# A hand-made list schedule with another rule for an engine's own results, new durations and a new set of urgencies

## The chip, the cores and the metric

The kernel runs on one core of a Trainium2 chip. The metric is the device time of one execution in microseconds. Of the kernel before, three runs gave 725.88, 728.35 and 729.00 us, so the median is 728.35 us. The profiled execution, from which all durations below come, took 728.77 us. Its span from the first to the last instruction is 727.0 us, and 1.77 us lie around it.

## What is computed

A packed attention feeds a feed-forward layer with an ELU in the middle. There are 8 batches, 8 heads, 576 tokens and 64 elements a head. 32 packed queries per head attend to the keys and values, and then the 576 queries attend to the packed result. The layer has 512 inputs, 2048 hidden units and 512 outputs, over all 4608 tokens.

```python
p_packed = sm_attn(p, k, v)                # softmax(scale * p k^T) v
out = sm_attn(q, p_packed, p_packed)
x = out.transpose(0, 2, 1, 3).reshape(B * S, H * D)
h = x @ w_in
g = np.where(h > 0.0, h, np.exp(np.minimum(h, 0.0)) - 1.0)
return g @ w_out
```

The inputs are float32, and the two weight matrices arrive as 64-bit words, which the kernel converts itself.

## The kernel before, in words

**The mathematics as it is tiled.** The second attention has only 32 keys a head, so the kernel multiplies its packed values with `w_in` first (`mstep`, matmuls on L800, evacuated as a high part on ScalarE and a low part on VectorE). The hidden layer of a token window is then a product of the softmax weights `a` with that `m`, both kept as a high and a low part, three matmuls for one product. The hidden matmuls stand on L1297 and L1304 (ordinary path) and on L1035 (Strassen path). ScalarE takes relu and exp of the result, VectorE joins them to the ELU, and the result `g` is split into a high and a low part again, for the output matmuls.

**Windows and steps.** Each batch has two windows. One takes 256 tokens, the other 320, of which 64 are kept aside as a leftover (`hb`) and written to memory. The leftovers of batches 0 to 3 and of 4 to 7 are read back later as two further sets of pairs ("rest"), beside the two windows of batch 7. A step is one window with one of the 16 slices f of 128 hidden units. The list `VISITS` says in which order batches 0 and 1 go through their steps, so that the first steps need only the first weights. A visit is a run of steps whose output is accumulated in PSUM. When it ends, the sums are copied out and stored, by an adding transfer of GpSimd's queue (L1447) where an earlier visit has stored already. From batch 2 on every window is one run of 16 steps. Counted so, batches 0 and 1 are steps 0 to 63, window (2, 0) is steps 64 to 79, and (2, 1) is steps 80 to 95.

**Two paths to the output.** Ordinary steps multiply a slice of `g` with its slice of `w_out` in six matmuls of 512 columns (L1400, L1401, L1403). From the window named in `S_FIRST` on, two slices go together as a pair, and a Strassen scheme does the pair with seven products in place of eight: 21 matmuls of 256 columns (L1191) where the ordinary way takes 12 of 512. For it VectorE forms sums of blocks of `g` (`sums`, three adds on L1117) and splits seven blocks and not four (L1126). The window's sums are put together at its end by a chain of VectorE adds (L1222). Sums of weight blocks are needed too: `strassen_weights(u)` makes them once for each of the eight pairs u (VectorE on L923, L929, L936, L939 and L956, casts on L308), stores them in memory, and each Strassen pair loads its four tiles again, 256 KB each. A pair named in `S_PLAINS` for its window is done the ordinary way with 12 matmuls inside the Strassen path.

**Who sets the order.** All work is declared as operations with an engine, a duration, dependencies, the buffers taken, and a number `prio`, which is a step plus or minus an offset. `schedule()` is a list scheduler. It keeps a clock of its own, and at each moment starts the ready operation of the lowest `prio` whose engine and buffers are free. The order that comes out is the program: every engine runs its instructions in that order, and the queue of SyncE (SP) issues its transfers in that order. The durations in the declarations have no other effect. `GAP` shortens the time for which an engine is taken, `LAG` lengthens the time until a result may be used. A result used by a later operation that can only run on the same engine counted as ready when that engine was free again, and every other result at its end with `LAG`.

**The offsets that the change touches.** `LI`, `LO` and `LM` say how many steps ahead of its first use a slice of `w_in`, a slice of `w_out` and an `mstep` become urgent. `FIRST` gives the order of the very first loads; the loads of k, v and q of one batch are chained in that order, and three weight slices fit in the staging ring. `T_ATT`, `T_ATT1`, `T_ATTS` time the six stages of a batch's attention, `TM` and `TMS` its four msteps, `T_S2` the second softmax half of batch 0. `T_SW` and `T_SW7` time the Strassen weights, `T_SL` the loads of their tiles, `T_SE` the adds at a window's end, `T_RL` and `T_RX` the loads and the output matmuls of the rest pairs, `T_HS` the stores of the leftovers. `LOOK` and `LOOK_S` say how many steps the output matmuls trail the hidden ones, and `STAY` how long PE stays with one kind of matmul.

Of the kernel before, what the change touches and what calls it, by code (L numbers as in the profile page):

```python
# [20 lines left out]
def packed_attention_elu_ffn(  # L21
# [51 lines left out]


    VISITS = [
# [4 lines left out]
    ]  # L80
    T_ATT = [8.5, 13.5, 10.5, 15.0, 16.0, 18.5]
    T_ATT1 = [-13.5, -9.5, -13.0, -6.5, -4.5, -13.5]
    LI = 6.5
    LO = 1.0
    LM = 3.0
    LOOK = 3.25
    TM = [22.5, 23.5, 25.0, 22.5]
    FIRST = "i3 i0 o0 k i2 v o1 q".split()
    T_S2 = 2.0
    STAY = 8  # L90
    SWITCH = 0.105
    F_PLAIN = 0
    H_PLAIN = [0, 1]
    T_WS = 33
    T_AS = 7
    S_PLAIN = []
    S_PLAINS = {
        (2, 0): [1], (2, 1): [0, 7], (3, 0): [4], (3, 1): [0], (4, 0): [0], (4, 1): [1],
        (5, 0): [], (5, 1): [0], (6, 0): [1], (6, 1): [1],
    }  # L100
    T_SW7 = 17
    T_ATTS = {3: [-3, 1.5, -4, 5, 12.5, 21.5], 4: [5.5, 5, 13.5, 8.5, 11.0, 25.5], 5: [-0.5, 0.5, -1.5, 6.5, 12.5, 21.0], 6: [5, 8.0, 14.5, 4.5, 17.0, 27.0], 7: [-4, -2, -2.5, 3, 14.5, 22.0]}
    TMS = {3: [21, 25, 25.5, 26.5], 4: [21.5, 19.5, 27.0, 27.0], 5: [23, 29, 33.0, 24.0], 6: [26.0, 15.5, 25.0, 27.0], 7: [19, 31, 30.0, 30.5]}
    T_RL = 7.0
    T_RX = 2.0
    T_HS = 29.0
    S_FIRST = (2, 0)
    T_SW = 17.5
    T_SL = 14.5
    T_SE = 12.5  # L110
    LOOK_S = 5.5

    class Ring:
# [47 lines left out]
        pass  # L161

    ops = []
    GAP = {"PE": 0.0, "DVE": -0.08, "ACT": -0.1, "DMA": 0.0, "POOL": 0.0, "CTL": 0.0}
    LAG = {"PE": 0.2, "DVE": 0.05, "ACT": 0.05, "DMA": 2.2, "POOL": 5.0, "CTL": 0.0}

    def op(prio, on, fn, deps=(), take=(), use=(), after=(), mode=None, lag=0):
        o = Op()
        o.lag = lag
        o.prio, o.on, o.fn, o.deps = prio, on, fn, [d for d in deps if d is not None]  # L170
        o.after = [d for d in after if d is not None]
        o.take, o.end, o.n, o.mode = list(take), None, len(ops), mode
        for b in list(take) + list(use):
            b.users.append(o)
        ops.append(o)
        return o

    def schedule():

        for o in ops:  # L180
            o.wait, o.ready, o.next = len(o.deps) + len(o.after), 0.0, []
        for o in ops:
            for d in o.deps:
                d.next.append((o, True))
            for d in o.after:
                d.next.append((o, False))
        todo = sorted(ops, key=lambda o: (o.prio, o.n))
        idle_at = {e: 0.0 for e in GAP}
        now, out, mode, converted = 0.0, [], None, 0
        conv = set(conv_ops)  # L190

        def engine_for(o):

            if o.wait or o.ready > now:
                return None
            for r in {id(b.ring): b.ring for b in o.take}.values():
                if not r.grant([b for b in o.take if b.ring is r], now):
                    return None

            spare = 2.0 * (converted < len(conv_ops))  # L200
            e = min(o.on, key=lambda e: max(idle_at[e], now) + o.on[e] + spare * (e == "DVE"))
            return e if idle_at[e] <= now else None

        while todo:
            for n, o in enumerate(todo[:400]):
                if o.wait or o.ready > now:
                    continue
                e = engine_for(o)
# [12 lines left out]
                idle_at[e] = now + cost + GAP[e]  # L221
                o.start, o.end = now, now + cost + LAG[e] + o.lag
                for x, needs in o.next:
                    x.wait -= 1
                    if needs:

                        x.ready = max(x.ready, idle_at[e] if list(x.on) == [e] else o.end)
                for r in {id(b.ring): b.ring for b in o.take}.values():
                    r.take([b for b in o.take if b.ring is r], now)
                out.append((o, e))  # L230
                todo.remove(o)
                converted += o in conv
                break
            else:
                ends = [o.end for o, _ in out[-400:] if o.end > now]
                ends += [t for t in idle_at.values() if t > now]
                assert ends, [(o.prio, o.on) for o in todo[:20]]
                now = min(ends)
        return out
# [168 lines left out]
    def attention(b, ts):  # L408
# [20 lines left out]
        if whole:  # L429
            x = ("k0", "q0")[b]  # L430
# [63 lines left out]
        for name, fn, bufs, t in (  # L494
# [12 lines left out]
        ld_k, ld_v, ld_q = lds["k"], lds["v"], prev_ld  # L507
        st.ld_q = ld_q
        e1T, tr_done = [], []
# [80 lines left out]
        o4s, o, t, free = [], None, ts[0], prev_b.tmp_last if b > 1 else None  # L590
        if b < S_FIRST[0] + 1:
            o1 = op(t, {"PE": 1.0}, s1, ld_k, take=ps1 + e1s, use=[p_b] + k_b, after=[free], mode=1)
            for g in range(G):
                o = op(t, {"DVE": 0.76}, lambda e, g=g: smax1(e, g), [o1], use=[ps1[g]], after=[o])
# [4 lines left out]
        else:  # L599
            kept, o1 = [], None  # L600
            for half in range(2):
# [9 lines left out]
                    t, {"ACT": 0.4}, lambda e, half=half, ps=ps, g=g: keep(e, half, ps, g), [o1],  # L611
                    use=[ps, e1s[g]],
                ) for g in range(G)]
            o = op(t, {"DVE": 0.26}, neg_both, [o])
            for g in range(G):
                o4s.append(op(
                    t, {"ACT": 0.9}, lambda e, g=g: sexp1_flat(e, g), [o] + kept[g::G], use=[e1s[g]],
# [40 lines left out]
                            start=(c == 0), stop=(c == NKC - 1),  # L658
                        )

        o = op(ts[2], {"PE": 0.85}, pv, ld_v + tr_done, take=[ps, pp_b], use=v_b + e1T, mode=2)
        done = []
        for g in range(G):
            def norm(e, g=g, ps=ps):
# [250 lines left out]
    def strassen_weights(u):  # L915
# [31 lines left out]
               w_split.get(f), w_split.get(f + 1)], take=[w_b, t_b], after=[run["w8"]])  # L947
        run["w8"] = x
        x = op(prio, {"DVE": 0.62}, t13, [x], use=[w_b, t_b])
        x = op(prio, {"DVE": 0.7}, t24, [x], use=[w_b, t_b])  # L950
        for n, b in enumerate(sw):
            def high(e, n=n, b=b):
                copy(e, b.t[:, :H], cut(t_b, n))
# [50 lines left out]
    def strassen_pair(i, b, win, f):  # L1004
# [128 lines left out]
            return g_b.all[:, x0:x0 + P]  # L1133

        if not plain:
            done = [op(i + 1, {"DVE": 0.95}, sums, done, use=[w8])]
        x = run["g"] = op(
            i + 1, {"ACT": 0.62 if plain else 0.95}, hi, done, take=[g_b], use=[w8], after=[run["g"]]
        )
# [359 lines left out]
```

## Time and profile before

| | |
|---|---|
| median of three runs | 728.35 us (725.88 to 729.00) |
| profiled execution | 728.77 us |
| its span | 727.0 us |
| PE busy | 680.1 us, 6060 matmuls |
| VectorE (DVE) busy | 610.8 us, 1311 instructions |
| ScalarE (ACT) busy | 460.4 us, 892 instructions |
| bytes moved | 167.80 MB, 231 GB/s mean |
| granted TensorE clock | 0.994 mean |

PE is the row of matmuls and PEld that of their weight loads. The profile's stretches give, for a piece of the span, each engine's busy time and the granted clock; the difference to the length of the piece is what the engine was idle. Matmuls overlap one another in the pipeline, so a matmul's own duration is longer than the distance to the next one, and the distance of starts is what it costs. Numbers in square brackets behind a row of the timeline are the idle time of that engine just ahead of it, and the instruction that ended it.

### The profile page before, as it was taken

How to read it: one execution, taken by the hardware profiler on the slowest of the kernel's cores; microseconds unless marked ns; L12 is line 12 of the kernel's file. 1: busy time of each engine (PE TensorE's matmuls, PEld its weight loads, DVE VectorE, ACT ScalarE, POOL GpSimd, SP SyncE). 2: the span in 40 equal slices, each digit the busy share in tenths (PEclk: the TensorE clock that was granted, in tenths of full speed). 3: DMA queues.
4: the chain of work that ended last, by engine and by line, in shares of the span. 5: the costliest groups of instructions: out<-in, count | busy, mean ns of one | idle time of the engine just before them, and what ended most of it. 6: DMA issues, size and time to landing. Idle time of an engine off the chain costs nothing. (4 is left out here: it accounts for less than half of the span.)

```text
span 727.0 us, 16122 instructions
## 1 busy us (share of the span) xinstructions
PE 680.1 (94%) x6060; PEld 592.3 (81%) x6060; DVE 610.8 (84%) x1311; ACT 460.4 (63%) x892; POOL 16.9 (2%) x24
## 2 busy tenths in 40 slices
PE   3698998999999999999999999999999999899996
PEld 2456777777779888898889889998799879899996
DVE  4899887999998987869977987879987989677874
ACT  6688999875777556655564567655564565454441
POOL 0000011010120000000000000000000000000000
PEclk9999999999999999999999999999999999999999
DMA  9856569388589976687778867997787758665763
GB/s 344 279 196 184 174 195 234 77 226 270 123 238 284 315 245 200 211 267 255 232 260 262 287 197 223 289 306 256 252 259 259 246 156 282 177 211 159 267 217 117
DMA packets 102799, 167.80 MB, mean 231 GB/s; under 512 B 26177, under 2 KB 35393, under 8 KB 102465
## 3 DMA queue, kind: packets, MB, share of 16 engines
q1 hardware_dynamic: 100128, 162.04, 68.8%
q0 software_dynamic: 2592, 4.72, 4.4%
q8 instruction: 48, 0.79, 0.4%
q14 instruction: 31, 0.25, 0.1%
HBM read 139.98 MB, written 26.74 MB: 229 GB/s over the span
## 5 line engine op out<-in xcount | busy, mean ns | idle before, releaser
L1191 PE MATMUL psum<-sw,g 128*128 128x256 f32 x1224 | 185.8, 284 | 0.3 <-DVE part L1222 0.3
L1191 PEld LDWEIGHTS psum<-sw,g 128*128 128x128 f32 x1224 | 162.7, 190 | 8.0 <-issue 7.4
L308 ACT CAST g<-w 128x896 fp32r<-128x896 f32 (+1 forms) x96 | 87.1, 907 | 77.9 <-DVE w L1117 59.2
L1126 DVE TENSOR_TENSOR g<-w,g 128x896 fp32r<-128x896 f32 (+1 forms) x96 | 100.0, 1044 | 28.0 <-ACT g L308 27.0
L1035 PE MATMUL psum<-a_hi,m_hi 128*128 128x256 f32 (+1 forms) x384 | 117.1, 305 | 6.6 <-DVE hb L1042 5.0
L1035 PE MATMUL psum<-a_lo,m_hi 128*128 128x256 f32 (+1 forms) x384 | 113.4, 295 | 0.0
L1035 PE MATMUL psum<-a_hi,m_lo 128*128 128x256 f32 (+1 forms) x384 | 113.4, 295 | 0.0
L1191 PE MATMUL psum<-wo_a,g 128*128 128x256 f32 (+1 forms) x552 | 93.2, 300 | 2.0 <-DVE hb L1042 2.0
L1117 DVE TENSOR_TENSOR w<-w 128x128 f32<-128x128 f32 (+1 forms) x258 | 86.8, 336 | 8.4
L1035 PEld LDWEIGHTS psum<-a_hi,m_hi 128*128 128x128 f32 x384 | 72.6, 189 | 20.6 <-issue 8.1
L1191 PEld LDWEIGHTS psum<-wo_a,g 128*128 128x128 f32 x552 | 78.3, 191 | 8.5 <-issue 3.6
L1191 PE MATMUL psum<-wo_b,g 128*128 128x256 f32 (+1 forms) x516 | 81.5, 286 | 0.0
L1191 PEld LDWEIGHTS psum<-wo_b,g 128*128 128x128 f32 x516 | 70.5, 189 | 3.5 <-issue 1.8
L1035 PEld LDWEIGHTS psum<-a_lo,m_hi 128*128 128x128 f32 x384 | 72.7, 189 | 0.2
L1035 PEld LDWEIGHTS psum<-a_hi,m_lo 128*128 128x128 f32 x384 | 72.6, 189 | 0.0
L1047 ACT ACTIVATE e<-psum 128x320 f32<-128x320 f32 x96 | 41.9, 436 | 39.3 <-PE psum L1035 34.3
L1042 DVE SCALAR_TENSOR_TENSOR w<-e,psum 128x256 f32<-128x256 f32 x96 | 39.8, 415 | 15.0 <-ACT e L1050 14.4
L1047 ACT ACTIVATE w<-psum 128x512 f32<-128x512 f32 x48 | 28.7, 597 | 29.5 <-PE psum L1035 12.7
L1050 ACT ACTIVATE e<-e 128x320 f32<-128x320 f32 x96 | 45.3, 471 | 2.9
L800 PE MATMUL psum<-w_in_sb,ppT 64*32 64x512 f32 (+1 forms) x640 | 36.1, 523 | 5.5 <-DVE w_in_sb L357 3.7
L813 DVE TENSOR_TENSOR m_lo<-psum,m_hi 128x1024 fp32r<-128x1024 f32 (+1 forms) x36 | 37.3, 1041 | 4.5 <-ACT m_hi L308 4.3
L1042 DVE SCALAR_TENSOR_TENSOR w<-w,psum 128x512 f32<-128x512 f32 x48 | 32.7, 682 | 9.8 <-ACT w L1050 9.3
(121 smaller groups left out, 1150.0 us busy)
## 6 DMA issues: line engine op xcount, KB each, us to landing
sw<-sw_dram SPq DMA_DIRECT2D x344, 256.0 KB, 3.7
raw<-in_w_in SPq DMA_DIRECT2D x16, 512.0 KB, 4.1
raw<-in_w_out SPq DMA_DIRECT2D x16, 512.0 KB, 5.1
kvq<-in_v SPq DMA_DIRECT2D x16, 512.0 KB, 5.2
out<-part SPq DMA_DIRECT2D x32, 256.0 KB, 3.1
sw_dram<-sw SPq DMA_DIRECT2D x32, 256.0 KB, 5.8
kvq<-in_kT SPq DMA_DIRECT2D x14, 576.0 KB, 4.9
kvq<-in_qT SPq DMA_DIRECT2D x14, 576.0 KB, 5.8
```

The lines of the kernel that those rows point to most:

```text
L308: (nc.scalar.copy if e == "ACT" else nc.vector.tensor_copy)(out=out, in_=in_)
L800: nc.tensor.matmul(ps.t[cols_of(pair), g, :w], lhsT=st.ppT.t[rows_of(g), pair, :], rhs=w_in_sb[rows_of(g), pair, c * FC + part * w:c * FC ...
L813: nc.vector.tensor_tensor(out=m_b[1].t[:, :, fs], in0=ps.t[:, :, :w], in1=m_b[0].t[:, :, fs].bitcast(F32), op=ALU.subtract,)
L1035: nc.tensor.matmul(ps, lhsT=m_b[p].t[:, g, o:o + P], rhs=st.a.t[q][:, g, cols], start=(n == 0), stop=(n == 3 * G - 1),)
L1042: nc.vector.scalar_tensor_tensor(out=out, in0=e_, scalar=-1.0, in1=ps, op0=ALU.add, op1=ALU.max)
L1047: nc.scalar.activation(out=out, in_=ps, func=AF.Relu, scale=-1.0)
L1050: nc.scalar.activation(out=x, in_=x, func=AF.Exp, scale=-1.0)
L1117: nc.vector.tensor_tensor(out=out, in0=x, in1=y, op=o)
L1126: nc.vector.tensor_tensor(out=g_b.all[:, 7 * P:(7 + b1 - b0) * P], in0=blocks(b0, b1), in1=g_b.all[:, :(b1 - b0) * P].bitcast(F32), op=ALU ...
L1191: nc.tensor.matmul(a.t[:, at * H:at * H + rhs.shape[-1]], lhsT=operand(blk, p), rhs=rhs, start=new and n == k == 0, stop=a.final == (u, mi ...
```

## The change

The scheduler loses its shorter rule for an engine's own results: every needed result now counts from its end with `LAG`. `LAG` of PE goes from 0.2 to 0.27 and `GAP` of DVE from -0.08 to -0.084. Four durations become longer: `neg_both` from 0.26 to 0.36, the product with the values (`pv`, L654) from 0.85 to 1.28, `t24` from 0.70 to 0.88, `sums` from 0.95 to 1.08. All constants named above but `LOOK_S`, `SWITCH`, `F_PLAIN`, `H_PLAIN` and `S_PLAIN` get other values. Three of these change what work is done. `S_FIRST` moves from (2, 0) to (2, 1), so window (2, 0) takes the ordinary path. `VISITS` has 14 visits and not 13: (1, 1, 0, 8) becomes two of four steps, and the order behind it is another. `S_PLAINS` lists other pairs, 9 for the windows from (2, 1) to (6, 1), where the list before has 9 for these and 1 for (2, 0). `FIRST` names nine loads and not eight.

```diff
     VISITS = [
-        (0, 0, 0, 4), (0, 1, 0, 4), (1, 0, 0, 4), (1, 1, 0, 8),
-        (0, 1, 4, 8), (1, 0, 4, 8), (0, 1, 8, 12), (0, 0, 4, 12),
-        (1, 0, 8, 12), (1, 1, 8, 16), (0, 1, 12, 16), (1, 0, 12, 16),
-        (0, 0, 12, 16),
+        (0, 0, 0, 4), (0, 1, 0, 4), (1, 0, 0, 4), (1, 1, 0, 4),
+        (1, 1, 4, 8), (1, 0, 4, 8), (0, 1, 4, 8), (0, 1, 8, 12),
+        (0, 0, 4, 12), (1, 0, 8, 12), (0, 1, 12, 16), (1, 1, 8, 16),
+        (1, 0, 12, 16), (0, 0, 12, 16),
     ]
-    T_ATT = [8.5, 13.5, 10.5, 15.0, 16.0, 18.5]
-    T_ATT1 = [-13.5, -9.5, -13.0, -6.5, -4.5, -13.5]
-    LI = 6.5
-    LO = 1.0
-    LM = 3.0
-    LOOK = 3.25
-    TM = [22.5, 23.5, 25.0, 22.5]
-    FIRST = "i3 i0 o0 k i2 v o1 q".split()
-    T_S2 = 2.0
-    STAY = 8
+    T_ATT = [11.5, 7.0, 12.0, 17.0, 11.5, 18.0]
+    T_ATT1 = [-20.0, -19, -16.0, -3.0, -18.5, -9.5]
+    LI = 5.0
+    LO = 2.5
+    LM = 2.0
+    LOOK = 4.0
+    TM = [22.0, 27.0, 34.5, 25.5]
+    FIRST = "q i3 o2 i2 i0 v k i1 o0".split()
+    T_S2 = -4.0
+    STAY = 9
...
-    T_WS = 33
-    T_AS = 7
+    T_WS = 21
+    T_AS = 3
     S_PLAIN = []
     S_PLAINS = {
-        (2, 0): [1], (2, 1): [0, 7], (3, 0): [4], (3, 1): [0], (4, 0): [0], (4, 1): [1],
-        (5, 0): [], (5, 1): [0], (6, 0): [1], (6, 1): [1],
+        (2, 0): [7], (2, 1): [0], (3, 0): [1], (3, 1): [0], (4, 0): [0], (4, 1): [1],
+        (5, 0): [0], (5, 1): [0], (6, 0): [], (6, 1): [1, 7],
     }
-    T_SW7 = 17
...
-    T_RL = 7.0
-    T_RX = 2.0
-    T_HS = 29.0
-    S_FIRST = (2, 0)
-    T_SW = 17.5
-    T_SL = 14.5
-    T_SE = 12.5
+    T_SW7 = 27
...
+    T_RL = 20.5
+    T_RX = 1.5
+    T_HS = 12.0
+    S_FIRST = (2, 1)
+    T_SW = 13.5
+    T_SL = 10.0
+    T_SE = 16.0
     LOOK_S = 5.5
...
-    GAP = {"PE": 0.0, "DVE": -0.08, "ACT": -0.1, "DMA": 0.0, "POOL": 0.0, "CTL": 0.0}
-    LAG = {"PE": 0.2, "DVE": 0.05, "ACT": 0.05, "DMA": 2.2, "POOL": 5.0, "CTL": 0.0}
+    GAP = {"PE": 0.0, "DVE": -0.084, "ACT": -0.1, "DMA": 0.0, "POOL": 0.0, "CTL": 0.0}
+    LAG = {"PE": 0.27, "DVE": 0.05, "ACT": 0.05, "DMA": 2.2, "POOL": 5.0, "CTL": 0.0}
...
                     if needs:
-
-                        x.ready = max(x.ready, idle_at[e] if list(x.on) == [e] else o.end)
+                        x.ready = max(x.ready, o.end)
...
-            o = op(t, {"DVE": 0.26}, neg_both, [o])
+            o = op(t, {"DVE": 0.36}, neg_both, [o])
...
-        o = op(ts[2], {"PE": 0.85}, pv, ld_v + tr_done, take=[ps, pp_b], use=v_b + e1T, mode=2)
+        o = op(ts[2], {"PE": 1.28}, pv, ld_v + tr_done, take=[ps, pp_b], use=v_b + e1T, mode=2)
...
-        x = op(prio, {"DVE": 0.7}, t24, [x], use=[w_b, t_b])
+        x = op(prio, {"DVE": 0.88}, t24, [x], use=[w_b, t_b])
...
-            done = [op(i + 1, {"DVE": 0.95}, sums, done, use=[w8])]
+            done = [op(i + 1, {"DVE": 1.08}, sums, done, use=[w8])]
```

`T_ATTS` and `TMS`, one row of offsets for each batch from 3 to 7, get other numbers throughout.

More of the change, by code (lines that the diff above doesn't have):

```diff
@@ L93, in packed_attention_elu_ffn @@
     H_PLAIN = [0, 1]
-    T_WS = 33
-    T_AS = 7
+    T_WS = 21
+    T_AS = 3
     S_PLAIN = []
     S_PLAINS = {
-        (2, 0): [1], (2, 1): [0, 7], (3, 0): [4], (3, 1): [0], (4, 0): [0], (4, 1): [1],
-        (5, 0): [], (5, 1): [0], (6, 0): [1], (6, 1): [1],
-    }
-    T_SW7 = 17
-    T_ATTS = {3: [-3, 1.5, -4, 5, 12.5, 21.5], 4: [5.5, 5, 13.5, 8.5, 11.0, 25.5], 5: [-0.5, 0.5, -1.5, 6.5, 12.5, 21.0], 6: [5, 8.0, 14.5, 4.5, 17.0, 27.0], 7: [-4, -2, -2.5, 3, 14.5, 22.0]}
-    TMS = {3: [21, 25, 25.5, 26.5], 4: [21.5, 19.5, 27.0, 27.0], 5: [23, 29, 33.0, 24.0], 6: [26.0, 15.5, 25.0, 27.0], 7: [19, 31, 30.0, 30.5]}
-    T_RL = 7.0
-    T_RX = 2.0
-    T_HS = 29.0
-    S_FIRST = (2, 0)
-    T_SW = 17.5
-    T_SL = 14.5
-    T_SE = 12.5
+        (2, 0): [7], (2, 1): [0], (3, 0): [1], (3, 1): [0], (4, 0): [0], (4, 1): [1],
+        (5, 0): [0], (5, 1): [0], (6, 0): [], (6, 1): [1, 7],
+    }
+    T_SW7 = 27
+    T_ATTS = {3: [-4, 2, -1.0, 7, 13.0, 21.5], 4: [-1.5, 7, 13.5, 3.0, 12.0, 24.0], 5: [-3.0, -2, -8.5, -5.5, 14.5, 28.0], 6: [7, 9, 13.5, 1.5, 13.0, 24.5], 7: [-3.5, -6, -5, 7.5, 14.5, 22.0]}
+    TMS = {3: [19, 29, 30.0, 30.5], 4: [22, 19.5, 26.0, 27.0], 5: [10.5, 29, 29.0, 31.0], 6: [23, 18.5, 26.0, 24.0], 7: [16.5, 35, 30.0, 31.0]}
+    T_RL = 20.5
[5 more added lines that the diff above has]
+    T_SE = 16.0
     LOOK_S = 5.5
```

## The prediction

> **What bounds the kernel now.** I read the page's head first, then the stretches, cut where the work changes its kind: the first hidden matmul at 29.72 us, the end of the weight conversion near 140, the first one of window (2, 0) at 207, the last windows. The columns are the stretch, its length, the busy times of PE, PEld, DVE, ACT and POOL, the granted clock, the DMA share and GB/s.
>
> ```profile
> span 727.0 us, 16122 instructions
> ```
>
> ```profile
> 0.00:29.72 29.72, 11.94 (x219) 6.67 (x219) 17.74 (x33) 16.43 (x32) 0.70 (x6) 0.94 0.89 326
> 29.72:60.00 30.28, 26.42 (x237) 18.07 (x238) 29.22 (x66) 24.76 (x60) 0.00 (x0) 1.00 0.57 179
> 60.00:140.00 80.00, 76.43 (x506) 60.56 (x505) 69.18 (x148) 75.10 (x172) 5.42 (x6) 1.00 0.66 183
> 140.00:207.00 67.00, 65.23 (x566) 49.52 (x565) 65.80 (x162) 46.22 (x115) 9.06 (x10) 1.00 0.75 207
> 207.00:237.60 30.60, 30.56 (x327) 27.71 (x319) 27.07 (x55) 22.84 (x42) 1.73 (x2) 1.00 0.90 265
> 237.60:262.00 24.40, 21.72 (x174) 19.00 (x173) 23.17 (x51) 13.57 (x24) 0.00 (x0) 1.00 0.88 305
> 262.00:620.00 358.00, 349.65 (x3259) 313.77 (x3257) 301.29 (x644) 215.55 (x384) 0.00 (x0) 1.00 0.77 246
> 620.00:626.00 6.00, 3.97 (x21) 3.85 (x20) 3.23 (x9) 2.04 (x4) 0.00 (x0) 0.72 0.61 173
> 626.00:700.00 74.00, 73.70 (x600) 72.83 (x599) 58.71 (x126) 36.98 (x55) 0.00 (x0) 1.00 0.66 208
> 700.00:727.00 27.00, 20.52 (x174) 20.31 (x173) 15.42 (x28) 6.96 (x10) 0.00 (x0) 0.96 0.43 150
> ```
>
> PE sets the end. It is idle 17.8 us before the first hidden matmul, 3.9 and 3.6 us in the next two stretches, 1.8 + 0.0 + 2.7 = 4.5 us from 140 to 262, 8.4 + 2.0 + 0.3 = 10.7 us from 262 to 700, and 6.5 us in the last stretch. That is all a new order can win, beside pauses hidden in the overlap of matmuls. VectorE decides where these waits lie: it is busy 65.8 of 67 us from 140 to 207. From 262 to 620 it has 57 us to spare, yet the waits of PE there end with it (columns: who waited for whom, us in total, times, longest):
>
> ```profile
> PE psum L1035 <- DVE hb L1042: 3.5, 7, 1.2
> PE psum L1191 <- DVE hb L1042: 2.0, 1, 2.0
> PE psum L558 <- DVE m_lo L813: 1.7, 1, 1.7
> ```
>
> So the late waits come from the place that an ELU (L1042) has in VectorE's queue, not from a want of VectorE.
>
> **1. Window (2, 0) leaves Strassen: more for PE, less for VectorE.** PE's cost is the distance of starts.
>
> ```profile
> 52.89 0.40 PE L1400 MATMUL psum<-wo_a,g 128*128 128x512 f32 x1
> ...
> 53.82 0.39 PE L1403 MATMUL psum<-wo_a,g 128*128 128x512 f32 x1
> ```
>
> ```profile
> 632.46 2.50 PE psum L1191 x21
> ```
>
> The two rows are the first and the last of five, so one matmul of 512 columns takes 0.93 / 4 = 0.233 us, and an ordinary pair 12 x 0.233 = 2.79 us. A Strassen pair takes 2.50 (a row of the chain). Seven pairs of (2, 0) change over, one was plain already: 7 x 0.29 = **+2.0 us** of PE work, which nothing hides. The plain pairs of the later windows are 9 before and after.
>
> VectorE's share, from the grouped lines, and the three adds of one pair from the timeline:
>
> ```profile
> L1126 DVE TENSOR_TENSOR g<-w,g 128x896 fp32r<-128x896 f32 x86 | 93.3, 1085 | 26.6 <-ACT g L308 25.6
> L1042 DVE SCALAR_TENSOR_TENSOR w<-w,psum 128x512 f32<-128x512 f32 x48 | 32.7, 682 | 9.8 <-ACT w L1050 9.3
> L1334 DVE TENSOR_TENSOR g<-e,g 128x256 fp32r<-128x256 f32 x64 | 26.6, 419 | 2.2 <-ACT g L308 2.0
> L1320 DVE SCALAR_TENSOR_TENSOR e<-e,psum 128x256 f32<-128x256 f32 x64 | 26.5, 416 | 4.2 <-ACT e L1317 3.6
> ```
>
> ```profile
> 211.83 1.08 DVE L1117 TENSOR_TENSOR w<-w 128x128 f32<-128x128 f32 x3
> ```
>
> A Strassen pair costs it 0.68 + 1.08 + 1.09 = 2.85 us, an ordinary one 2 x (0.42 + 0.42) = 1.67, so 7 x 1.18 = 8.2 us go. ScalarE gets six shorter calls a pair for three longer ones; its 7.8 us of idle time from 207 to 237.6 cover that, and without that cover it would be late in a window whose PE has no idle time. 28 loads of 256 KB go as well. What this returns is seen where (2, 0) passes into (2, 1):
>
> ```profile
> 242.66 1.07 DVE L1117 TENSOR_TENSOR w<-w 128x128 f32<-128x128 f32 x3
> 244.34 0.39 PE L1035 MATMUL psum<-a_hi,m_hi 128*128 128x320 f32 x1 [1.51 <-DVE hb L1042]
> ```
>
> ```profile
> 254.26 2.34 DVE L1222 TENSOR_TENSOR part<-part,psum 128x512 f32<-128x512 f32 x4 [0.44 <-PE psum L1191]
> 256.05 0.41 PE L1035 MATMUL psum<-a_hi,m_hi 128*128 128x320 f32 x1 [1.09 <-DVE part L1222]
> ```
>
> The adds of a pair, then the closing adds of (2, 0) stand ahead of what PE needs: 1.5 + 1.1 us. An ordinary window closes with two copies and no such chain. I take **-2.6 us**; the bounds are 0, where the Strassen weights take the place, and -4.5, all of PE's idle time from 140 to 262.
>
> **2. The Strassen weights later** (`T_SW` 17.5 to 13.5 steps, one window later in all). Their first instruction, and the first and the last row of one set:
>
> ```profile
> 138.50 1.22 DVE L923 TENSOR_TENSOR w<-wo_a 128x1024 f32<-128x1024 f32 x1
> ...
> 214.93 1.22 DVE L923 TENSOR_TENSOR w<-wo_a 128x1024 f32<-128x1024 f32 x1
> ...
> 218.03 1.43 DVE L956 TENSOR_TENSOR sw<-w,sw 128x256 fp32r<-128x256 f32 x4
> ```
>
> A set is 218.03 + 1.43 - 214.93 = 4.5 us, eight sets 36 us. After the change other work goes ahead of them. Room: from 207 to 237.6 VectorE is busy 27.1 us; less seven Strassen pairs (20.0) and the set in it (4.5), with seven ordinary pairs (11.7), that is 14.3 of 30.6 + 2.0 us, so four sets fit. I cost the delay at nothing; what it costs beyond four is the slower rival.
>
> **3. The start.** The row of the first wait, and what ended it:
>
> ```profile
> 21.21 0.67 ACT L329 ACTIVATE mi<-raw 128x512 f32<-128x512 f32 x1 [0.40 <-DMA raw<-in_w_in]
> 25.25 1.11 PE L800 MATMUL psum<-w_in_sb,ppT 64*32 64x256 f32 x16 [3.71 <-DVE w_in_sb L357]
> 27.20 0.78 DVE L749 STREAM_TRANSPOSE k<-tmp 128x576 f32<-128x576 f32 x1
> 29.72 1.99 PE L1297 MATMUL psum<-k,m_hi 128*128 128x256 f32 x8 [0.79 <-ACT m_hi L308]
> ```
>
> Slice i1 of `w_in` is loaded last, its conversion starts at 21.21, and the first mstep waits for it until 25.25. In the new order i1 has one slice fewer ahead of it: 512 KB at the 326 GB/s of this stretch, 1.6 us by estimate. The softmax half that the first hidden matmul needs as well ends at 27.98, so 29.72 can come down to 28 at best. i0 and o0 now load later, but are needed no sooner than i1 and the first output. k still comes behind three slices, so its arrival stays. I take **-1.5 us**; bounds -3.7 (the whole wait) and +1.6 (one slice late).
>
> **4. One visit more.**
>
> ```profile
> PE psum L1400 <- ACT part L308: 1.5, 3, 0.9
> ```
>
> Three changes of visit cost PE 1.5 us between 60 and 262, so one more costs **+0.5**; bounds 0 and +0.9. Its two copies fall on a ScalarE that is busy 75 of 80 us from 60 to 140; its two adding transfers go to GpSimd's queue, which is busy 5.4 us there.
>
> **5. The rule, the durations, the offsets.** No trace row has an order in it that was not yet made, so this is bounded. Dependent and independent neighbours on VectorE:
>
> ```profile
> 22.33 0.75 DVE L714 TENSOR_REDUCE mx<-tmp 128x18 f32<-128x576 f32 x1
> 23.11 0.76 DVE L717 TENSOR_TENSOR tmp<-tmp,mx 128x576 f32<-128x576 f32 x1
> 23.79 0.68 DVE L347 SCALAR_TENSOR_TENSOR mi<-mi,rd 128x512 uint32<-128x512 uint32 x1
> ```
>
> The subtraction needs the maximum and starts 0.03 us after its end; L347 needs nothing of the subtraction and starts 0.08 us before its end. The rule now charges this 0.11 us, and `sums` its traced 1.08. So the list sees VectorE's chains nearly as long as they are, and knows better when an ELU gets late. At stake are the 10.7 us of PE's idle time from 262 to 700 and the clock behind the longest wait: the granted clock is 0.72 over the 6 us from 620, which is 1.7 us lost. Of these 12.4 us I take a third, **-4.1 us**, because the errors put right (0.1 to 0.2 us each) are much smaller than the waits (1 to 2 us each). Bounds: -8, two thirds; and +4, new waits of the same size elsewhere.
>
> The page "VectorE: DVE Perf Modes" of the Trainium skill, "The DRAIN you can't avoid", speaks against this step: the next operation starts only once the pipe is empty, and a semaphore costs nothing extra. By it putting other work between would win nothing. The three rows, 0.03 us after against 0.08 us before, do not agree.
>
> A wait for SP or a moved transfer costs nothing here: offsets of tile loads, leftover stores and rest loads (`T_SL`, `T_HS`, `T_RL`) move transfers past each other on SP, whose DMA engines are busy 66 to 77% from 262 to 700. If that cover went, a late tile would show as PE waiting for a DMA, which no row after the first k does. The last stretch stays: its end follows the last matmul.
>
> **The sum.** +2.0 - 2.6 - 1.5 + 0.5 - 4.1 = -5.7 us. The span is 727.0, with 1.77 us around it the profiled run is 728.77, so 723.1. The median of the runs shown, 728.35, is 0.42 lower: **722.7 us**.
>
> **The rivals.**
> - No change: step 5 wins nothing, its waits only move, and i1 does not decide the start. Then 728.35 + 2.0 - 2.6 + 0.5 = 728.3. For it: the waits are many times longer than the corrections. Against it: VectorE has 57 us to spare from 262 to 620, so there is room for a better order. The skill's rule above would do the same to step 5 alone: 722.7 + 4.1 = 726.8; its chance is 0.05, within this case.
> - Slower: the Strassen weights crowd (2, 1). If all eight sets still stand when (2, 0) begins, four are left at its end, 18 us of VectorE work ahead of or among the pairs of (2, 1). There VectorE is busy 23.2 of 24.4 us up to 262, so hardly any of it is free; -2.6 turns into a wait. With half of the 18 us on PE's path: 728.35 + 2.0 + 0.5 - 1.5 + 9 = 738. It decides from the fifth set left at 207. Against it: the list starts a set when VectorE is free, and the trace has the first set at 138.50.
> - Much faster: every bound at its good end but the start's, 722.7 - 1.9 - 3.9 - 0.5 = 716.4.
>
> **How the numbers follow.** A measurement here tells about 0.5% (3.6 us) from no change. The forecast has 0.44 and the much faster case 0.10, together 0.54 for faster; no change 0.28; slower 0.18. The range goes from 712, somewhat below the much faster case, to 733, which leaves most of the slower rival out: about 0.05 below and 0.13 above.
>
> **What would show it.** Right: about 63 matmuls fewer (7 x 9), VectorE busy near 602 us, some 7 MB less moved, no Strassen row before (2, 1), the waits on L1222 and L1042 near 245 to 256 gone, the first L1297 near 28 us, under 8 us of PE idle time from 262 to 700, no stretch at a lower clock after the start. Wrong: sets of L923 still running in (2, 1) with PE waiting; PE's idle time after 262 as large as before; a new wait over 2 us followed by half clock; the first hidden matmul after 30 us.

## The result, and the profile after

The changed kernel takes 704.08 us (702.06 to 706.43, four runs) against 728.67 of the kernel before (725.88 to 730.92, four runs). The ratio is 0.9665, with a 95% interval from 0.9616 to 0.9715. That is 24.6 us less, where 5.7 were forecast, and below the forecast's lower bound of 712. The head of the page after the change:

```profile
span 704.6 us, 15947 instructions
## 1 busy us (share of the span) xinstructions
PE 675.3 (96%) x5991; PEld 590.3 (84%) x5991; DVE 587.8 (83%) x1323; ACT 449.1 (64%) x897; POOL 18.5 (3%) x26
```

The stretches of the kernel before, cut at the first hidden matmuls of step 0 (29.7), of step 64 (207.1), of step 96 (280.7) and of step 255 (702.3). The columns are those of the prediction's table:

```profile
0.00:29.70 29.70, 11.94 (x219) 6.67 (x219) 17.72 (x33) 16.41 (x32) 0.70 (x6) 0.94 0.89 326
29.70:207.10 177.40, 168.18 (x1306) 128.15 (x1306) 164.32 (x372) 146.19 (x345) 14.48 (x16) 1.00 0.68 191
207.10:280.70 73.60, 70.88 (x650) 64.44 (x642) 64.06 (x140) 47.77 (x89) 1.73 (x2) 1.00 0.87 272
280.70:702.30 421.60, 410.93 (x3748) 375.03 (x3741) 351.52 (x745) 243.88 (x421) 0.00 (x0) 1.00 0.75 239
702.30:727.00 24.70, 18.22 (x155) 18.01 (x153) 13.19 (x23) 6.19 (x9) 0.00 (x0) 0.96 0.40 139
```

The changed kernel, cut at the same steps:

```profile
0.00:34.90 34.90, 17.00 (x229) 8.48 (x230) 17.89 (x38) 19.88 (x39) 0.69 (x6) 0.98 0.86 307
34.90:205.80 170.90, 165.36 (x1298) 129.46 (x1297) 156.99 (x364) 138.03 (x335) 16.08 (x18) 0.99 0.69 190
205.80:276.80 71.00, 71.00 (x585) 61.66 (x584) 60.31 (x158) 43.26 (x98) 1.75 (x2) 1.00 0.59 187
276.80:680.80 404.00, 403.70 (x3732) 372.71 (x3731) 339.19 (x742) 241.82 (x420) 0.00 (x0) 1.00 0.79 250
680.80:704.60 23.80, 18.19 (x155) 17.98 (x153) 13.38 (x24) 6.16 (x9) 0.00 (x0) 0.96 0.44 145
```

Of the 22.4 us between the two spans, 17.6 come from steps 96 to 255, the late stretch: 421.6 against 404.0. Its work is nearly the same (3748 and 3732 matmuls). PE's idle time there falls from 10.7 to 0.3 us, and its busy time falls by 7.2 us on top of it. Some 1.7 us of that is the lower clock behind the wait at 620 us, which the prediction had counted; cut into pieces of six us, the changed kernel's late stretch has a granted clock of 1.00 in each. The other 5.5 us of the old loss stood in no idle time: by the distances of starts it was pauses between matmuls, hidden by their overlap. The start goes the other way, 34.9 for 29.7. What PE waits for in the middle of the late stretch (285 to 680 us), as who waited for whom, total, times and longest, is this one row, where the kernel before has nine, 10.3 us together:

```profile
PE psum L1190 <- ACT e L1049: 0.3, 1, 0.3
```

### The profile page after: what moved, and what is told of

Its sections match the earlier page's. It is cut to its first block, busy times and chain, and to the rows that moved or that the text cites. A ratio compares the mean times of both kernels' runs of the same rounds, so it can differ in the third digit from the quotient of the medians.

```text
span 704.6 us, 15947 instructions
## 1 busy us (share of the span) xinstructions
PE 675.3 (96%) x5991; PEld 590.3 (84%) x5991; DVE 587.8 (83%) x1323; ACT 449.1 (64%) x897; POOL 18.5 (3%) x26
## 4 chain that ended last, share of the span: by engine, by line
PE 83%; ACT 7%; DVE 4%; DMA 3%; issue 2%; SPq 0%; DVEq 0%; ACTq 0%
PE psum L1190 37%; PE psum L1034 20%; PE psum L1303 5%; PE psum L799 4%; PE psum L1399 3%; PE psum L1400 3%; PE psum L1402 3%; DMA raw<-in_w_out 2%; PE psum L653 2%; PE psum L627 1%; PE psum L698 1%; DMA k<-in_kT 1%; ACT e L1316 1%; ACT e L1310 1%; ACT g L307 1%
## 5 line engine op out<-in xcount | busy, mean ns | idle before, releaser
L1190 PE MATMUL psum<-sw,g 128*128 128x256 f32 x1140 | 173.2, 283 | 0.0
L1190 PEld LDWEIGHTS psum<-sw,g 128*128 128x128 f32 x1140 | 151.4, 189 | 8.7 <-DMA sw<-sw_dram 4.7
L1125 DVE TENSOR_TENSOR g<-w,g 128x896 fp32r<-128x896 f32 (+1 forms) x88 | 91.7, 1042 | 23.5 <-ACT g L307 23.3
L1034 PE MATMUL psum<-a_hi,m_hi 128*128 128x320 f32 (+1 forms) x352 | 105.9, 301 | 0.0
L1034 PE MATMUL psum<-a_lo,m_hi 128*128 128x320 f32 (+1 forms) x352 | 104.4, 297 | 0.0
L1034 PE MATMUL psum<-a_hi,m_lo 128*128 128x320 f32 (+1 forms) x352 | 104.4, 297 | 0.0
L1116 DVE TENSOR_TENSOR w<-w 128x128 f32<-128x128 f32 (+1 forms) x237 | 79.1, 334 | 6.0
L1310 ACT ACTIVATE e<-psum 128x256 f32<-128x256 f32 (+1 forms) x80 | 33.0, 413 | 21.4 <-PE psum L1303 17.7
L1319 DVE SCALAR_TENSOR_TENSOR e<-e,psum 128x256 f32<-128x256 f32 x80 | 32.9, 411 | 9.5 <-ACT e L1316 9.5
L1303 PE MATMUL psum<-a_hi,m_hi 128*128 128x256 f32 (+1 forms) x128 | 37.8, 296 | 2.4 <-DVE e L1319 2.4
```

What stands on the lines that cost most here:

```text
L1034: nc.tensor.matmul(ps, lhsT=m_b[p].t[:, g, o:o + P], rhs=st.a.t[q][:, g, cols], start=(n == 0), stop=(n == 3 * G - 1),)
L1116: nc.vector.tensor_tensor(out=out, in0=x, in1=y, op=o)
L1125: nc.vector.tensor_tensor(out=g_b.all[:, 7 * P:(7 + b1 - b0) * P], in0=blocks(b0, b1), in1=g_b.all[:, :(b1 - b0) * P].bitcast(F32), op=ALU ...
L1190: nc.tensor.matmul(a.t[:, at * H:at * H + rhs.shape[-1]], lhsT=operand(blk, p), rhs=rhs, start=new and n == k == 0, stop=a.final == (u, mi ...
L1303: nc.tensor.matmul(ps_b.t[:, :n_tok], lhsT=m_b[x].t[:, g, o:o + P], rhs=st.a.t[y][:, g, cols], start=(n == 0), stop=(n == 3 * G - 1),)
L1310: nc.scalar.activation(out=e_b.t[:, :n_tok], in_=ps_b.t[:, :n_tok], func=AF.Relu, scale=-1.0)
```

## The experiments

Lines in the changed kernel stand one lower than before. Below, "start" is the time of the first hidden matmul, "early" the distance from it to the first one of step 96, "late" from there to the first one of step 255, each read from the profiled execution's timeline. What follows the last of these is 24 to 25 us in all kernels. Ratios are to the kernel before on the same chip. The times of a profiled execution vary up to step 64: old_new_rule and rule_dummy have VectorE's and ScalarE's work in one order until then, and reach step 64 at 205.0 and 207.4 us; the changed kernel and new_strassen20, which agree up to about 163 us, have starts of 34.9 and 32.2, and step 64 at 205.8 and 202.1. So a difference of under 4 us in "start" and "early" says little.

| kernel | median us | ratio (95%) | start | early | late |
|---|---|---|---|---|---|
| before | 728.67 | | 29.7 | 251.0 | 421.6 |
| changed | 704.08 | 0.9665 (0.9616 to 0.9715) | 34.9 | 241.8 | 404.0 |
| old_new_rule | 709.99 | 0.9728 (0.9710 to 0.9747) | 31.6 | 243.6 | 408.7 |
| old_new_model | 710.67 | 0.9737 (0.9723 to 0.9752) | 32.2 | 250.7 | 403.5 |
| new_old_model | 737.94 | 1.0104 (1.0074 to 1.0134) | 29.4 | 258.8 | 420.9 |
| new_old_rule | 733.07 | 1.0044 (1.0023 to 1.0064) | 30.5 | 256.9 | 420.4 |
| rule_dve_only | 715.78 | 0.9824 (0.9791 to 0.9857) | 31.2 | 249.9 | 407.7 |
| rule_act_only | 731.48 | 1.0036 (1.0013 to 1.0059) | 30.7 | 255.7 | 418.9 |
| rule_pe_only | 733.18 | 1.0064 (1.0039 to 1.0090) | 30.9 | 251.7 | 424.0 |
| rule_dve_act | 710.63 | 0.9751 (0.9710 to 0.9791) | 32.1 | 241.9 | 408.8 |
| rule_dve_pe | 717.85 | 0.9853 (0.9811 to 0.9896) | 33.6 | 253.5 | 407.7 |
| old_charge | 723.97 | 0.9943 (0.9914 to 0.9972) | 30.1 | 255.0 | 412.8 |
| old_spread | 721.88 | 0.9909 (0.9881 to 0.9936) | 30.6 | 250.8 | 413.5 |
| old_charge_spread | 716.72 | 0.9827 (0.9788 to 0.9865) | 30.1 | 251.3 | 406.9 |
| rule_dummy | 725.52 | 0.9952 (0.9932 to 0.9973) | 33.3 | 246.9 | 419.0 |
| rule_dummy_listed | 718.07 | 0.9836 (0.9807 to 0.9865) | 33.8 | 247.3 | 410.5 |
| new_strassen20 | 709.93 | 0.9748 (0.9694 to 0.9802) | 32.2 | 245.6 | 403.8 |
| new_old_visits | 706.48 | 0.9706 (0.9667 to 0.9745) | 33.6 | 241.6 | 404.6 |
| new_hold | 705.03 | 0.9686 (0.9645 to 0.9727) | 31.3 | 244.6 | 405.6 |
| new_split_sums | 706.78 | 0.9678 (0.9647 to 0.9709) | 34.7 | 241.5 | 404.9 |

### The rule or the offsets?

The first four kernels put the new list (rule, durations) and the new choices (offsets, loads, visits, plain pairs) together in other ways. In old_new_rule, the kernel before gets the one line:

```diff
-                        x.ready = max(x.ready, idle_at[e] if list(x.on) == [e] else o.end)
+                        x.ready = max(x.ready, o.end)
```

> The kernel before with the new readiness rule alone; offsets, loads, plain pairs and durations stay. Theory RULE (the old order let VectorE's dependent instructions stand too early, and the rule alone puts that right): 710 to 718 us, with VectorE pairs of neighbours that depend on each other (gap of 10 to 60 ns) down from 454 towards 300. Theory OFFSETS (the newly chosen offsets carry the gain): 725 to 732 us.

In old_new_model it also gets `LAG`, `GAP` and the four durations as in the change.

> The kernel before with the rule, LAG, GAP and the four durations new; all offsets stay old. Theory RULE with true durations: 706 to 716 us. Theory OFFSETS: 724 to 734 us, since offsets chosen for another list are now out of tune.

new_old_rule is the changed kernel with that one line put back, and new_old_model the changed kernel with the line, `LAG`, `GAP` and the durations put back.

> The changed kernel with the old rule, LAG, GAP and durations; the offsets, (2, 0) on the ordinary path, visits and plain pairs stay new. Theory RULE: most of the gain goes, 718 to 728 us. Theory OFFSETS: most of it stays, 703 to 711 us.

> The changed kernel with the old readiness rule alone put back. Theory RULE: 714 to 726 us, VectorE's dependent neighbours back above 400. Theory OFFSETS: 703 to 711 us.

The rule alone, with every old offset, gives 709.99, 20.2 us less than the 730.15 that the kernel before took beside it: most of the 24.6. The new choices without the rule lose 0.4%, and 1.0% without the durations too, which is worse than either theory expected. The late stretch sorts the kernels by the rule alone: 420.4 to 421.6 without it, 403.5 to 408.7 with it. Of the durations' effect one sees 5 us in the late stretch (408.7 to 403.5) and 7 us lost again early (243.6 to 250.7); in the total the two cancel. So the new choices are worth 5 to 7 us on top of the new list (0.9737 to 0.9665 by the ratios, 710.67 to 704.08 by the medians), all of them before step 96 (250.7 to 241.8, less the later start), and nothing without it. Which of the many new choices bring this was not separated, beyond the two tried further below.

What the rule does is seen in VectorE's neighbours. In the kernel before, from its timeline of VectorE:

```profile
303.15 0.41 DVE L1042 SCALAR_TENSOR_TENSOR w<-e,psum 128x256 f32<-128x256 f32 x1
303.60 1.08 DVE L1117 TENSOR_TENSOR w<-w 128x128 f32<-128x128 f32 x3
```

and in the changed kernel:

```profile
304.23 0.42 DVE L1041 SCALAR_TENSOR_TENSOR w<-e,psum 128x256 f32<-128x256 f32 x1 [1.50 <-ACT e L1049]
304.57 0.21 DVE L1041 SCALAR_TENSOR_TENSOR hb<-e,psum 128x64 f32<-128x64 f32 x1
304.70 1.07 DVE L1116 TENSOR_TENSOR w<-w 128x128 f32<-128x128 f32 x3
```

Before, the adds follow the ELU that they need, 0.04 us after its end. Now the leftover's ELU, which nothing on VectorE waits for there, stands between, and both neighbours start 0.08 us before the end of the one ahead. Counted over the trace (gap to the instruction ahead 10 to 60 ns), VectorE has 454 dependent neighbours before, 314 in old_new_rule, 284 in the changed kernel, and 449 again in new_old_rule. Of the 454, 204 stand inside the adds of a pair (two in each of 102 sets), which are one operation of the list; no rule can part them.

### Whose results?

In these five, `e` in the old line is excepted for the engines named, so that their own results follow the new rule and the others the old one. For VectorE alone:

```diff
-                        x.ready = max(x.ready, idle_at[e] if list(x.on) == [e] else o.end)
+                        x.ready = max(x.ready, idle_at[e] if list(x.on) == [e] and e != "DVE" else o.end)
```

> The kernel before, the new readiness rule for results of VectorE alone (ScalarE's and PE's own results keep the old one). Theory VECTORE (the gain of the rule comes from VectorE's chains): 708 to 715 us. Theory SCALARE or PE: 722 to 732 us.

> The kernel before, the new rule for results of ScalarE alone (relu and then exp, above all). Theory VECTORE: 724 to 732 us, VectorE's dependent neighbours still above 430. Theory SCALARE: 708 to 718 us.

> The kernel before, the new rule for results of PE alone, which in this kernel are the output matmuls of batches 0 and 1. If the rule's parts add up (all 710, VectorE alone 715.8, ScalarE alone 731.5 of 729): 721 to 726 us, gained before step 96. If they do not add up and VectorE's part needs the others: 727 to 732 us.

> The kernel before, the new rule for results of VectorE and ScalarE, PE's own left as before. If ScalarE's part helps once VectorE's chains are right: 708 to 712 us, the 6 us gained before step 96. If it is PE's part: 714 to 718 us.

> The kernel before, the new rule for results of VectorE and PE, ScalarE's own left as before. The counterpart: 708 to 712 us if PE's part brings the rest before step 96, 714 to 718 us if it is ScalarE's.

VectorE's results alone give 1.8% and the whole late gain of the rule (407.7, against 408.7 in old_new_rule). It is a little past the range of theory VECTORE, since the early part stays at 249.9. ScalarE's alone and PE's alone lose a little. Yet ScalarE's on top of VectorE's bring the rest, early: 249.9 to 241.9 in the profiled runs, 715.78 to 710.63 in the medians, though the two intervals just touch. PE's add nothing to either. The parts do not add up, so undoing one at a time would have misled here.

### What of the rule: the truer clock, or the room between?

The rule does two things at once. The list knows that a chain is longer, and it has a free moment behind each operation in which something else goes first. These kernels keep the old rule and have each by itself. old_charge counts the later start, but leaves the choice as it was:

```diff
                 cost = o.on[e]
+                if e in ("DVE", "ACT") and last.get(e) in o.deps:
+                    cost += LAG[e] - GAP[e]
+                last[e] = o
```

> The kernel before with the old rule, but where the list puts an operation of VectorE or ScalarE straight behind one that it needs, it counts the later start in its clock (0.13 and 0.15 us). The list then knows the true length of a chain, yet has no reason to put other work into it. Theory CLOCK (the gain comes from the list knowing when an ELU is late): 708 to 718 us. Theory GAPS (the gain is the time that VectorE no longer stands between an instruction and its dependent): 723 to 733 us, dependent neighbours still above 430.

old_spread leaves the clock as it was, but takes another operation first:

```diff
+                if e == "DVE" and last.get(e) in o.deps:
+                    for x in todo[n + 1:n + 400]:
+                        if x.prio >= o.prio + 4:
+                            break
+                        if list(x.on) == [e] and last[e] not in x.deps and engine_for(x) == e:
+                            o = x
+                            break
+                last[e] = o
                 cost = o.on[e]
```

> The kernel before with the old rule and the old clock, but where the next VectorE operation needs the one just placed, the list takes another ready VectorE operation first, if one of a priority less than 4 steps later is there. Theory GAPS: 708 to 720 us, dependent neighbours of VectorE below 350. Theory CLOCK: 722 to 734 us.

old_charge_spread has both pieces.

> The kernel before with the old rule and both halves of it put in by hand: the list counts the later start of a dependent neighbour, and takes another ready VectorE operation in between. Alone they gave 724.0 and 721.9 us of 728.9, and 8.8 and 8.1 us in steps 96 to 255. Theory BOTH (these two are what the rule does on VectorE): 711 to 717 us, steps 96 to 255 in 406 to 410 us. Theory SAME WAITS (each removes the same waits): 719 to 724 us, steps 96 to 255 in 412 to 414.

Neither theory held alone: 0.6% and 0.9%, each about half of the late gain (412.8 and 413.5, from 421.6). The kernel old_spread kept 370 dependent neighbours, where below 350 were expected. Together they give 406.9 late and 716.72 in all, which is VectorE's part of the rule (407.7 and 715.78) within its intervals. So the two together are as much as the rule on VectorE. They are not the same order: 376 dependent neighbours are left, against 321 in rule_dve_only, and old_charge counts ScalarE's later start as well. That the rule is these two things and no more is therefore likely, but not shown.

### Is it VectorE's time, or what the list does not know of it?

Each dependent neighbour costs 0.11 us of VectorE, so old_spread also made VectorE's work shorter. rule_dummy gives time back: old offsets, new rule, and ahead of each pair's adds three memsets of eight useless columns. The output stays as it was.

```diff
         def sums(e):
+            for _ in range(3):
+                nc.vector.memset(spare, 0.0)
```

> The kernel before with the new rule, and three tiny memsets of no use ahead of each pair's three sums, which the list does not know of (output as it was). They give VectorE back the time that the rule saved: about 0.15 to 0.2 us at each of 86 pairs, 12 to 16 us in all. Theory TIME (VectorE's time was the bound): the time is given back, 718 to 726 us. Theory ORDER (with the right order there is slack on VectorE): 709 to 714 us.

rule_dummy_listed is the same, with `{"DVE": 1.12}` and not 0.95 for `sums`, so that the list counts them.

> The memset run again (old offsets, new rule, three useless memsets ahead of each pair's sums), but the list is told of them: the sums count 1.12 in place of 0.95 us. Theory TIME (VectorE's time itself was the bound): as before, 720 to 728 us. Theory CLOCK (what the list did not know of did the harm): 709 to 716 us.

The late stretches of the two, first unlisted and then listed, beside the 408.80 us of old_new_rule with 343.32 us of VectorE:

```profile
280.20:699.20 419.00, 412.93 (x3764) 374.42 (x3763) 353.74 (x1006) 245.64 (x421) 0.00 (x0) 1.00 0.77 242
```

```profile
281.10:691.60 410.50, 406.45 (x3721) 372.04 (x3720) 349.42 (x995) 243.12 (x425) 0.00 (x0) 1.00 0.76 245
```

```profile
275.10:683.90 408.80, 407.44 (x3765) 373.28 (x3764) 343.32 (x751) 245.44 (x421) 0.00 (x0) 1.00 0.79 248
```

Unlisted, the memsets make VectorE 10.4 us busier there and the stretch 10.2 longer. Listed, VectorE is 6.1 us busier and the stretch 1.7 longer. In the late stretch, then, VectorE does have time to spare, but hardly for work that the list does not know of. The listing is not complete: from its first memset on, a set of adds takes 1.32 us in the trace, 0.37 more than the 0.95 of the one list and 0.20 more than the 1.12 of the other. Without memsets it takes 1.07, 0.12 more than the list has it in old_new_rule. The late stretch follows this error: 408.7, 410.5, 419.0. The memsets are three at each of 102 sets, and not of 86 as expected. The first one runs at 212 us, so the later start and the later step 64 (207.4 and 206.6, against 205.0) are not theirs. Steps 64 to 95 take 72.8 and 74.5 us, against 70.2, so there they do cost time, listed or not. The total of the listed run, 718.07, lies between the two theories. The two runs differ in VectorE's busy time too, so the split is not exact.

### The window (2, 0), the visits, the start, and what bounds it now

new_strassen20 is the changed kernel with `S_FIRST = (2, 0)`.

> The changed kernel with window (2, 0) back on the Strassen path. PE has 2.0 us less matmul work, VectorE 8.2 us more. Theory RELIEF (the lighter VectorE in steps 64 to 95 pays for the matmuls, as the prediction had it): 705 to 709 us, with the time from step 64 to step 96 longer than in the changed kernel. Theory FLOOR (with the new rule VectorE no longer holds PE there): 700 to 703 us.

It takes 709.93, and it needs 75.8 us for steps 64 to 95 against 71.0. RELIEF is right in direction, and by more than thought. The intervals of the two ratios overlap, so its size in the total is not settled. Nor is it a matter of VectorE's load alone: old_new_rule has (2, 0) on the Strassen path too, with the old offsets, and needs 70.2 us for these steps, with PE idle for 0.04 us of them:

```profile
204.99:275.15 70.16, 70.12 (x635) 64.86 (x627) 62.80 (x143) 44.80 (x81) 1.73 (x2) 1.00 0.85 262
```

new_old_visits is the changed kernel with the 13 visits of before.

> The changed kernel with the 13 visits of before in their old order. If the new visits carry what the offsets add to the rule (about 6 us): 708 to 714 us, lost before step 64. If not: 702 to 707 us.

706.48 and early parts that are alike (241.6 and 241.8): the visits do not carry the gain.

The start of the changed kernel, from its timeline:

```profile
27.03 0.75 DVE L726 TENSOR_REDUCE sm<-tmp 128x18 f32<-128x576 f32 x1 [0.15 <-ACT tmp L722]
27.11 3.11 PE L516 MATMUL psum<-kvq,p 64*32 64x288 f32 x32
...
30.27 0.76 DVE L526 TENSOR_REDUCE mx<-psum 128x1 f32<-128x576 f32 x1 [2.49 <-PE psum L516]
30.94 0.17 DVE L729 TENSOR_SCALAR sm<-sm 128x18 f32<-128x18 f32 x1
...
33.33 0.77 DVE L748 STREAM_TRANSPOSE k<-tmp 128x576 f32<-128x576 f32 x1
...
34.92 2.31 PE L1296 MATMUL psum<-k,m_hi 128*128 128x256 f32 x5
```

The sum (L726) of batch 0's first half needs nothing but itself for its next step (L729), but the list has put the maximum of batch 1 (L526) between. On the chip L526 waits for PE's L516, which takes 3.11 us here, and the whole half stands behind it. That this order is the rule's doing shows new_old_rule, the same offsets without it: there L729 follows at once.

```profile
25.69 0.74 DVE L726 TENSOR_REDUCE sm<-tmp 128x18 f32<-128x576 f32 x1
26.46 0.18 DVE L729 TENSOR_SCALAR sm<-sm 128x18 f32<-128x18 f32 x1
...
27.77 0.78 DVE L748 STREAM_TRANSPOSE k<-tmp 128x576 f32<-128x576 f32 x1
```

The length of the wait is not the order's alone. new_strassen20 has the order of the changed kernel here, and its L526 waits 0.61 us:

```profile
27.58 0.76 DVE L526 TENSOR_REDUCE mx<-psum 128x1 f32<-128x576 f32 x1 [0.61 <-PE psum L516]
```

new_hold orders L526 behind that half:

```diff
-                o = op(t, {"DVE": 0.76}, lambda e, g=g: smax1(e, g), [o1], use=[ps1[g]], after=[o])
+                o = op(t, {"DVE": 0.76}, lambda e, g=g: smax1(e, g), [o1], use=[ps1[g]],
+                       after=[o] + (prev_b.af_done[:1] if b == 1 else []))
```

> The changed kernel with one ordering more: the first maximum of batch 1 stands on VectorE only after the first softmax half of batch 0 is done. In the changed kernel it stands ahead of that half's reciprocal and waits 2.5 us for PE at half clock. Theory HEAD (that wait delays all that follows): first hidden matmul at 29 to 31 us in place of 34.9, time 699 to 702 us. Theory COVER (steps 0 to 64 are bound by VectorE and ScalarE anyway): first hidden matmul earlier, time 703 to 706 us.

The first hidden matmul comes at 31.3 and the time stays, 705.03. The eight steps behind it take 32.2 us, where they take 26.2 in the changed kernel: COVER. So the time does not hang on the first hidden matmul.

Last, the three adds of a pair as three operations of the list, from the changed kernel:

```diff
-            done = [op(i + 1, {"DVE": 1.08}, sums, done, use=[w8])]
+            for part, cost in enumerate((0.3, 0.43, 0.3)):
+                done = [op(i + 1, {"DVE": cost}, lambda e, part=part: sums(e, part), done, use=[w8])]
```

> The changed kernel with the three adds of a pair (L1116) as three operations of the list, 0.30, 0.43 and 0.30 us, so that other VectorE work can stand between them. 190 of the 284 dependent neighbours that are left on VectorE are these. If VectorE's time is still the bound, 100 or more go, 11 us or more of VectorE time, and with 0.6 us for one: 696 to 700 us. If PE is the bound now (it has 0.3 us of idle time from 277 to 620 us): 701 to 706 us.

The dependent neighbours fall from 284 to 178, as meant, and VectorE's busy time by 6.3 us, from 587.8:

```profile
PE 676.0 (96%) x5991; PEld 590.3 (84%) x5991; DVE 581.5 (82%) x1326; ACT 446.3 (63%) x894; POOL 18.6 (3%) x26
```

The time does not: 706.78, late stretch 404.9. Less work for VectorE wins nothing there any more, and PE is idle for 0.7 us of that stretch: PE is the bound there now. None of these versions beats the changed kernel.

## Why the prediction was wrong, point by point

**1. Window (2, 0).** Right in direction under the new offsets, but the reason is not shown. +2.0 of PE and -2.6 were 0.6 us less; the profiled runs of new_strassen20 and the changed kernel show 4.8 less in steps 64 to 95 (75.8 against 71.0). The waits at 244 and 256 are gone: PE has no idle time from 205.8 to 276.8. But they are gone in old_new_rule as well, with the window still on the Strassen path (70.2 us, 0.04 us of PE's idle time). So the rule alone, with the old offsets, removes the waits whose end the prediction expected of the lighter window. The trace has 69 matmuls fewer; 63 were worked out, since the one plain pair of (2, 0) had been taken for 12 matmuls and had 18 (a window whose list does not name pair 0 does its plain pairs with 6 matmuls of 512 columns and 12 of 256).

**2. The Strassen weights.** Right in its cost of nothing, but the delay that it allowed for did not come. A line's view of the changed kernel (count, shortest, middle and longest duration in ns, first and last start) has the sets starting where they did, from 139.9 to 214.0 us. So the slower rival, which needed five sets left when (2, 0) begins, did not come up:

```profile
L922 DVE TENSOR_TENSOR w<-wo_a x4: 1214/1216/1225, 139.9 to 214.0; 128x1024 f32<-128x1024 f32 x4
L922 DVE TENSOR_TENSOR w<-wo_b x4: 1206/1216/1219, 165.0 to 199.7; 128x1024 f32<-128x1024 f32 x4
```

**3. The start.** Wrong in sign: 34.9 us and not 28 (34.7 and 32.2 in new_split_sums and new_strassen20, whose order is the same there). i1 did come earlier (the first mstep runs at 24.40 and not 25.25), but something else became last: the head of VectorE's queue. It costs next to nothing in the end, as new_hold shows.

**4. The visit.** +0.5 was too small to be seen; new_old_visits neither shows nor excludes it.

**5. The rule, the durations, the offsets.** This is the step that failed: "Of these 12.4 us I take a third, -4.1 us, because the errors put right (0.1 to 0.2 us each) are much smaller than the waits (1 to 2 us each). Bounds: -8, two thirds". The late stretch gave 17.6, more than the whole stake. Two things were wrong in it. The first is the share, a third. Nearly the whole stake was won: PE's idle time there fell by 10.4 us, and the lower clock, 1.7 us of the stake, is gone. The second is the stake itself. It was sized from PE's idle time and that clock, and left out the pauses within busy time, which the prediction names but does not size; they gave the other 5.5 us.

The third rested on setting a small error for each neighbour against one wait, as if it acted alone. It does not: the late stretch had 310 dependent neighbours. 137 of them stood between operations of the list, each 0.11 us later than the list had it, some 15 us in all; the rule left 51 of them. 173 stood inside the adds of a pair, which the list had 0.13 us too short at each of some 86 sets, some 11 us more; these the new duration of `sums` puts right, and old_new_model, with all the new durations, shows 5.2 us of late gain on top of the rule. How this adds up in the order was not followed instruction by instruction. But that it does is shown from two sides: counting it (old_charge) and avoiding it (old_spread) each brought half of the gain, and 10.4 us of VectorE work that the list does not know of made the late stretch 10.2 us longer, while 6.1 us that it knows of in good part made it 1.7 longer.

VectorE was forecast at 602 us and is busy 587.8. Beside the 8.2 us of window (2, 0), 170 dependent neighbours went, 14 of them inside that window's adds. Where the other 156 became independent ones, each overlaps the instruction ahead by 0.08 us: some 12 us by estimate, from the counts and the rows above.

The reading that the late waits come from the ELU's place in the queue "not from a want of VectorE" held: listed memsets cost the late stretch little. But the prediction put rule, durations and offsets into one term, and so could not see that most of it is one line of code, and that the new offsets by themselves lose. The rival of no change named the size of the corrections as its evidence, which is the same error.

The page "VectorE: DVE Perf Modes" of the Trainium skill, "The DRAIN you can't avoid", says that the next operation does not start until the pipe is empty; by that sentence alone step 5 would be worth nothing. The runs do not agree with it: 0.04 us after the end for a dependent, 0.08 us before it for another, and a gain where the list is made to know. The same section adds that a next operation that is not held starts earlier, and gives no time for it.

## What to carry to other kernels

Where a program is ordered by a list with a clock of its own, a small error that recurs is to be multiplied by its count before it is weighed against a wait. Let a result used on its own engine count from its end; and choose offsets only then, because those chosen for one list can be worse than the old ones under another. Size what a better order can win on a pipelined engine from the distance of starts, not from its idle time alone.

## What was not expected of the hardware

Two neighbours on VectorE cost 0.11 us more when the second needs the first (0.03 or 0.04 us after the end, against 0.08 before it), and there were 454 such places in one execution. The first matmuls of batch 1's attention (L516) took 3.11 us in the changed kernel, where the same 32 took 2.18 in the kernel before, and VectorE stood 2.5 us behind them. In both they start in groups 0.48 us apart, four groups before and six after, because half of them wait for their weights until 28.07 us, which by the profile come with the load of k. The first row is of the kernel before, the second of the changed one:

```profile
26.11 2.18 PE L517 MATMUL psum<-kvq,p 64*32 64x288 f32 x32
```

```profile
28.07 0.23 PEld L516 LDWEIGHTS psum<-kvq,p 64*32 64x32 f32 x16 [0.77 <-DMA kvq<-in_kT]
```

The kernel before has a granted clock of 0.50 over that row, and of 1.00 six us earlier, where 32 matmuls of the same size (L699) start 0.24 us apart. In the changed kernel the profile shows a granted clock of 1.00 from 27.11 to 30.27 at the slow pace of 0.48. So the half clock in the expectation of new_hold is seen in the pace of the matmuls, but not in the clock that the profile gives.
